# A recurrence and an ELU network in one launch: the output gate by tanh, smaller first loads, and a planner with other numbers

## The chip, the core and the metric

The kernel runs on one core of a Trainium2 chip. The core has a matrix engine (TensorE, PE in the profile; its weight loads are PEld), a vector engine (VectorE, DVE), an activation engine (ScalarE, ACT), a general one (GpSimd, POOL) and SyncE (SP), which here issues every DMA. The metric is device time of one launch in microseconds (us); less is better. Each engine works through its own queue in order; between engines the order is kept by semaphores.

## The reference

Four batches of eight heads run a gated recurrence over 768 positions of 40 channels; its output, 3072 rows of 320, goes through a two-layer network with an ELU. Cut to what matters:

```python
for t in range(S):
    m_new = np.maximum(f_gate[:, :, t] + m, i_gate[:, :, t])
    f_stab = np.exp(f_gate[:, :, t] + m - m_new)
    i_stab = np.exp(i_gate[:, :, t] - m_new)
    C = f_stab[..., None, None] * C + i_stab[..., None, None] * np.einsum('bhd,bhe->bhde', vt, kt)
    n = f_stab[..., None] * n + i_stab[..., None] * kt
    h_tilde = np.einsum('bhde,bhe->bhd', C, qt)
    denom = np.maximum(np.abs(nq), 1.0)          # nq = n . q, per head
    o = 1.0 / (1.0 + np.exp(-o_gate[:, :, t]))
    y[:, :, t] = o * h_tilde / denom
...
h = x @ w_in                                     # (3072, 320) @ (320, 2048)
g = np.where(h > 0.0, h, np.exp(np.minimum(h, 0.0)) - 1.0)
return g @ w_out                                 # (3072, 2048) @ (2048, 320)
```

The weights arrive in double precision.

## The kernel before

**Tiles.** The 768 positions are cut into six chunks of 128, and tile n is chunk c = n // 4 of batch b = n % 4, 24 tiles in all. Within a chunk the recurrence is done as attention with decays (`attention(n)`): scores of keys and queries (`products`, L597), a matrix w of decays, which for the first two chunks comes from sums of logs that PE spreads into a PSUM buffer h (`spread`, L628 to L638) and an Exp on ACT, and for later chunks from a scan on DVE (L645); w times scores (L662); outputs in PSUM (`outputs`, L682 to L700) with the state C of earlier chunks. `gate_chunk(c)` prepares the gates of one chunk for all batches, mostly on DVE. The end of a tile is a chain: Abs of the normalizer (L733, ACT), max with 1 and reciprocal (L737, L738, DVE), the sigmoid of the output gate times 1/den (L742, DVE or POOL), times the output (L746, DVE), a copy, a transpose on PE (`turn`, L763), and a split of the result into a high and a low part (xh, L769; xl, L776 or L780), because the network's matmuls work in a shorter format and sum several products. The sigmoid itself is three activations in place over 320 columns (L615): Exp of -x, Ln of 1 + that, Exp of the negative.

**Network.** `ffn` works on blocks of two or three tiles. A step is 128 of the 2048 hidden columns: eight matmuls of the first layer into an h buffer (L816), Relu and Exp on ACT (L824, L827), add and max on DVE (L829), a split (L832 on ACT, L834 on DVE or POOL), and three matmuls a tile of the second layer (L843). Steps run in a fixed order. A PSUM pool has two h buffers, used by steps, by spreads and by some weight conversions.

**Weights.** `conversion(i)` turns a piece of double-precision words, i = 0 to 17 (c0, c1, ... in the order below), into high and low parts: a load into one of three wide buffers (L322), two passes on ACT (L327, L332), three on DVE (L336, L341, L346), an add on POOL (L351), the high part by a copy on ACT (L357), the low part by DVE, POOL or by PE and a copy (L361, L369 to L373). The wide buffer is free after the add on POOL. The first step of the first block needs c0, c1 and c2 (its second layer c3), steps 2 and 3 need c4, steps 4 on c5 to c7.

**Order.** Nothing is scheduled by the chip or by the compiler. A planner (`Plan`) takes every operation with the engines that may do it, a cost in us on each, the buffers that it touches and a rank, simulates engines, one DMA queue and the pools, and writes the operations out in the order in which its simulation starts them, each on the engine on which it would end first. Ready operations go by rank, then by the longest tail of costs behind them. Its constants are HOP (delay from one engine to another), RATE (bytes per us of the DMA queue), LAND (delay of a landing) and DEEP (how far SP's issues may run ahead of the queue). FIRST gives ranks 0, 1, 2, ... to tiles (t) and conversions (c); those not named in it get a small rank from the step that needs them. An operation with "port" in its costs shares a port between DVE and POOL.

## Time and profile before

| | |
|---|---|
| median of 3 runs | 480.05 us (475.24 to 480.37) |
| profiled execution | 479.09 us, of which the span on the core is 477.1 us |
| mean granted clock of TensorE | 0.981 |
| instructions | 13768 |
| moved by DMA | 52.83 MB, 39389 packets |

The span runs from the first to the last instruction of one profiled execution. Busy time is the time in which an engine had an instruction in work; matmuls are pipelined, and at a granted clock below 1.00 the same work is busy for longer. A line such as L816 is a line of the kernel; one line may issue on different engines.

### The profile page before, as it was taken

Reading aid. Unit: us, or ns where it says so; the run is one execution under the profiler, and the core shown is the slowest. Engines: PE = TensorE matmul, PEld = TensorE weight load, DVE = VectorE, ACT = ScalarE, POOL = GpSimd, SP = SyncE. Lnnn points to the kernel's source line nnn. Section 1 sums busy time; section 2 is a strip of 40 time slices with the busy share of each in tenths; the row PEclk is TensorE's granted clock in tenths of the full one; section 3 lists DMA queues with packets and bytes.
Section 4 is the critical chain, followed back from the end, with each engine's and each line's share of the span. In section 5 each row is a group of like instructions: output and inputs, shape, how many; then the busy total and the mean of one; then the engine's idle time right before and its main releaser. Section 6 shows DMA issues by size and latency. Waiting matters only on the chain.

```text
span 477.1 us, 13768 instructions
## 1 busy us (share of the span) xinstructions
PE 456.9 (96%) x5692; PEld 428.4 (90%) x5692; DVE 347.8 (73%) x729; ACT 303.1 (64%) x743; POOL 89.5 (19%) x103
## 2 busy tenths in 40 slices
PE   5977999999999989999999999999999999999996
PEld 3645889899999989999989999999999999999996
DVE  7897899997869899638995768648875475456543
ACT  5886788897876556646465546655546564645764
POOL 2421244433213131003040122102110010000000
PEclk9796999999999999999999999999999999999999
DMA  8777465534143394113642334404432030100000
GB/s 261 259 225 233 134 214 170 153 116 153 41 137 97 105 278 138 43 40 98 185 144 71 101 94 134 133 3 139 140 101 82 1 101 1 43 1 3 28 1 27
DMA packets 39389, 52.83 MB, mean 111 GB/s; under 512 B 2880, under 2 KB 31264, under 8 KB 39328
## 3 DMA queue, kind: packets, MB, share of 16 engines
q1 hardware_dynamic: 39328, 51.97, 35.2%
q8 instruction: 44, 0.72, 0.6%
q14 instruction: 17, 0.14, 0.1%
HBM read 46.56 MB, written 5.39 MB: 109 GB/s over the span
## 4 chain that ended last, share of the span: by engine, by line
PE 80%; DVE 10%; DMA 3%; issue 2%; ACT 2%; POOL 1%; SPq 1%; DVEq 0%; ACTq 0%
PE h L816 34%; PE acc L843 32%; PE ps_a L597 4%; PE ps_a L690 3%; PE ps_a L682 2%; DMA wide<-in_w_in 2%; PE ps_a L763 1%; DMA w<-f_d 1%; PE h L628 1%; PE ps_a L700 1%; PE h L632 1%; PE h L638 1%; DVE w L645 1%; DMA bb<-b_d 1%; DVE gl L834 1%
## 5 line engine op out<-in xcount | busy, mean ns | idle before, releaser
L816 PE MATMUL h<-xh,w 128*128 128x384 f32 (+1 forms) x720 | 179.1, 323 | 0.4 <-ACT e L827 0.2
L843 PE MATMUL acc<-w,gh 128*128 128x320 f32 x768 | 173.4, 312 | 0.1
L843 PEld LDWEIGHTS acc<-w,gh 128*128 128x128 f32 x768 | 127.8, 188 | 2.4 <-ACT gh L832 0.3
L816 PEld LDWEIGHTS h<-xh,w 128*128 128x128 f32 x720 | 125.6, 189 | 2.7 <-DVE e L829 1.0
L829 DVE SCALAR_TENSOR_TENSOR e<-e,h 128x384 f32<-128x384 f32 (+1 forms) x144 | 72.5, 505 | 69.8 <-ACT e L827 69.2
L843 PE MATMUL acc<-w,gl 128*128 128x320 f32 x384 | 118.7, 309 | 0.4 <-DVE gl L834 0.4
L824 ACT ACTIVATE e<-h 128x384 f32<-128x384 f32 (+1 forms) x144 | 65.4, 454 | 78.0 <-PE h L816 74.9
L816 PE MATMUL h<-xl,w 128*128 128x384 f32 (+1 forms) x432 | 112.0, 318 | 0.0
L832 ACT CAST gh<-e 128x384 fp32r<-128x384 f32 (+1 forms) x144 | 67.7, 473 | 35.1 <-DVE e L829 34.0
L834 DVE TENSOR_TENSOR gl<-e,gh 128x384 fp32r<-128x384 f32 (+1 forms) x122 | 66.3, 547 | 32.1 <-ACT gh L832 30.2
L816 PEld LDWEIGHTS h<-xl,w 128*128 128x128 f32 x432 | 76.9, 189 | 0.0
L827 ACT ACTIVATE e<-e 128x384 f32<-128x384 f32 (+1 forms) x144 | 70.5, 490 | 4.0
L843 PEld LDWEIGHTS acc<-w,gl 128*128 128x128 f32 x384 | 72.0, 188 | 0.9 <-DVE gl L834 0.8
L834 POOL TENSOR_TENSOR gl<-e,gh 128x384 fp32r<-128x384 f32 (+1 forms) x22 | 24.4, 1115 | 109.0 <-ACT gh L832 95.6
L645 DVE TENSOR_TENSOR_SCAN w<-w,ident 128x512 f32<-128x512 f32 x32 | 39.1, 1225 | 4.6 <-DMA w<-f_d 4.6
L615 ACT ACTIVATE vko<-vko 128x320 f32<-128x320 f32 x72 | 33.5, 467 | 7.7 <-DMA vko<-in_vko 7.2
L597 PE MATMUL ps_a<-qk 40*128 40x128 f32 x384 | 31.0, 304 | 6.4 <-DMA qk<-in_qk 5.1
L351 POOL TENSOR_TENSOR narrow<-narrow,wide 128x512 int32<-128x512 int32 (+1 forms) x18 | 26.5, 1474 | 55.5 <-DVE narrow L346 25.9
L597 PEld LDWEIGHTS ps_a<-qk 40*128 40x128 f32 x384 | 25.9, 204 | 11.6 <-DMA qk<-in_qk 5.1
L662 DVE TENSOR_TENSOR w<-ps_a,w 128x512 f32<-128x512 f32 x48 | 31.6, 682 | 3.1 <-PE ps_a L597 2.7
L690 PE MATMUL ps_a<-vko,w 128*32 128x41 f32 x1536 | 20.3, 207 | 0.0
L690 PEld LDWEIGHTS ps_a<-vko,w 128*32 128x32 f32 x1536 | 18.6, 114 | 1.2 <-issue 1.1
(104 smaller groups left out, 413.9 us busy)
## 6 DMA issues: line engine op xcount, KB each, us to landing
vko<-in_vko SPq DMA_DIRECT2D x24, 484.0 KB
qk<-in_qk SPq DMA_DIRECT2D x24, 448.0 KB
w<-f_d SPq DMA_DIRECT2D x32, 256.0 KB
wide<-in_w_out SPq DMA_DIRECT2D x8, 640.0 KB
wide<-in_w_in SPq DMA_DIRECT2D x8, 512.0 KB
out<-os SPq DMA_DIRECT2D x24, 160.0 KB
bb<-b_d SPq DMA_DIRECT2D x40, 80.0 KB
sum<-os SPq DMA_DIRECT2D x8, 160.0 KB
```

Of the source, the lines that this page charges most:

```text
L597: nc.tensor.matmul(ps(two, P, HH, L)[:, j, :], kt[rows, j, :], qt[rows, j, :], start=True, stop=True,)
L615: lambda e, fn=fn, kw=kw: nc.scalar.activation(v3()[2], v3()[2], fn, **kw), (), (KS,))
L645: nc.vector.tensor_tensor_scan(a, a, ident4.rearrange("p h t -> p (h t)"), 0.0, op0=ALU.mult, op1=ALU.add)
L662: lambda e, half=half: nc.vector.tensor_mul(w(half), ps(half, P, HH, L), w(half)),
L690: nc.tensor.matmul(y[r, h, :], w()[:, i, r], va()[:, h, :], start=not opened, stop=(i == H - 1), skip_group_check=True,)
L816: nc.tensor.matmul(h(), a[g][:, fs], m, start=(i == 0), stop=(i == len(prods) - 1))
L824: op(act(N), lambda e, h=h, ff=ff: nc.scalar.activation(ff("e"), h(), AF.Relu, scale=-1.0), (KHP,), (KE,))
L827: lambda e, ff=ff: nc.scalar.activation(ff("e"), ff("e"), AF.Exp, scale=-1.0), (), (KE,))
L829: lambda e, h=h, ff=ff: nc.vector.scalar_tensor_tensor(out=ff("e"), in0=ff("e"), scalar=-1.0, in1=h(), op0=ALU.add, op1=ALU.max),
L832: op(act(N), lambda e, ff=ff: nc.scalar.copy(ff("gh", F32R), ff("e")), (KE,), (KG,))
L834: lambda e, ff=ff: eng[e].tensor_sub(ff("gl", F32R), ff("e"), ff("gh", F32R).bitcast(F32)),
L843: nc.tensor.matmul(acc(a), x[:, sl], bw[g][:, j, :], start=(f == f0 and i == 0), stop=(f == f1 - 1 and i == 2),)
```

## The change

The sigmoid is written as (1 + tanh(x/2)) / 2: one activation in place of three. The 1 is added in the instruction that multiplies by the output, the 1/2 goes into the denominator as a factor of 2, and the multiplication by 1/den comes last, on the product. The table set that ACT preloads is another one. For tiles of chunk 0 the queries and keys, which lie in 112 rows of which 80 hold data (0 to 39 and 64 to 103), are loaded as two transfers of 40 rows. The copies of xh and xl, and the copy of the low part in a conversion by PE, may go to ACT or DVE. The planner has other constants, a factor on PE's costs in the first 45 us (COLD), a hop by engine, other costs for some operations, and FIRST names another order.

```diff
-    HOP = 0.1
+    HOP = {"PE": 0.19, "POOL": 0.06, "DVE": 0.04, "ACT": 0.04, "SP": 0.04}
+    COLD = ((11.5, 1.9), (18.0, 1.0), (25.0, 1.9), (45.0, 1.25))
     LAND = 1.6
-    RATE = 235e3
-    DEEP = 3.0
+    RATE = 275e3
+    DEEP = 6.0
...
-                    end = t + o.engines[best]
+                    cost = o.engines[best]
+                    if best == "PE":
+                        cost *= next((x for until, x in self.COLD if t < until), 1.0)
+                    end = t + cost
...
-    FIRST = "t0c0c4t1c1c5t2t4c3c7c11c9"
+    FIRST = "t0c0c2c3t1t2t3t4c4c1"
...
-                op(act(n), lambda e, lo=lo: nc.scalar.copy(lo, T("h", ("lower", i), P, 4 * L)[:, 0:n]),
+                op(act(n) | two_ps(n), lambda e, lo=lo: copy(e, lo, T("h", ("lower", i), P, 4 * L)[:, 0:n]),
...
-        nc.scalar.preload_act_table_set("natural_log_exp_and_others")
+        nc.scalar.preload_act_table_set("exp_and_others")
...
-        op({"SP": 0.4}, lambda e: nc.sync.dma_start(t[0:R3], qk[b, c]),
-           (), (("qk", n, 0), ("qk", n, 1)), nbytes=R3 * 2 * HH * L * 4)
+        for two, rows in enumerate(ROWS if c == 0 else [slice(0, R3)]):
+            op({"SP": 0.4}, lambda e, rows=rows: nc.sync.dma_start(t[rows], qk[b, c, rows]),
+               (), (("qk", n, two),) if c == 0 else (("qk", n, 0), ("qk", n, 1)),
+               nbytes=(rows.stop - rows.start) * 2 * HH * L * 4)
...
-        for fn, kw in ((AF.Exp, dict(scale=-1.0)), (AF.Ln, dict(bias=1.0)), (AF.Exp, dict(scale=-1.0))):
-            op(act(H * D),
-               lambda e, fn=fn, kw=kw: nc.scalar.activation(v3()[2], v3()[2], fn, **kw), (), (KS,))
+        op(act(H * D), lambda e: nc.scalar.activation(v3()[2], v3()[2], AF.Tanh, scale=0.5), (), (KS,))
...
-            nc.vector.tensor_scalar_max(den(), den(), 1.0)
+            nc.vector.tensor_scalar(den(), den(), 1.0, 2.0, op0=ALU.max, op1=ALU.mult)
...
-        op({"port": 1, "DVE": 0.3}, denominators, (), (("den", n),))
+        op({"port": 1, "DVE": 0.41}, denominators, (), (("den", n),))
+
+        def gated():
+            return xf()[:, 0 : H * D].rearrange("p (h d) -> p h d", d=D)
+
+        op({"DVE": 0.49},
+           lambda e: nc.vector.scalar_tensor_tensor(
+               out=gated(), in0=v3()[2], scalar=1.0, in1=y3()[:, :, 0:D], op0=ALU.add, op1=ALU.mult),
+           (KY, KS), (("xf", n),))
         op(two_in(H * D),
-           lambda e: eng[e].tensor_mul(v3()[2], v3()[2], den().to_broadcast([P, H, D])),
-           (("den", n),), (KS,))
-
-        def result(e):
-            nc.vector.tensor_mul(
-                xf()[:, 0 : H * D].rearrange("p (h d) -> p h d", d=D), y3()[:, :, 0:D], v3()[2]
-            )
-
-        op({"DVE": 0.49}, result, (KY, KS), (("xf", n),))
+           lambda e: eng[e].tensor_mul(gated(), gated(), den().to_broadcast([P, H, D])),
+           (("den", n),), (("xf", n),))
...
-        op(act(3 * L), lambda e: nc.scalar.copy(xs("h"), ps("tp", P, 3, L)),
+        op(act(3 * L) | two_ps(3 * L), lambda e: copy(e, xs("h"), ps("tp", P, 3, L)),
            (KTP,), (KX + ("h", slot),))
```

The lines left out change single costs: `products` on PE from 1.25 to 1.16, `outputs` from 1.6 to 1.38, the split of the logs on DVE from 1.8 to 2.2, small fills and copies on DVE from 0.08 to 0.17, and others of that size.

## Rows read from the trace of the kernel before

**Rows 1.** The profile's page, its head and its list of busy times: busy microseconds of each engine, its share of the span, and its number of instructions.

```profile
span 477.1 us, 13768 instructions
...
PE 456.9 (96%) x5692; PEld 428.4 (90%) x5692; DVE 347.8 (73%) x729; ACT 303.1 (64%) x743; POOL 89.5 (19%) x103
```

**Rows 2.** Busy time by stretches of the span. Columns: the stretch in us, its length, then for each engine the busy us in it and its instructions, the clock of TensorE that was granted (1.00 is full speed), the mean busy share of the 16 DMA engines, and GB/s.

```profile
5.00:11.80 6.80, 6.42 (x35) 4.05 (x36) 4.66 (x17) 3.88 (x8) 0.12 (x1) 1.00 1.04 336
18.70:25.50 6.80, 6.76 (x122) 5.00 (x122) 5.65 (x14) 4.81 (x13) 2.93 (x3) 0.51 0.52 166
25.50:39.10 13.60, 8.26 (x137) 5.09 (x136) 12.93 (x34) 12.14 (x30) 3.39 (x3) 0.99 0.76 237
39.10:49.40 10.30, 8.67 (x134) 7.05 (x134) 7.52 (x19) 5.65 (x14) 2.36 (x3) 0.51 0.82 237
5.00:50.00 45.00, 36.49 (x567) 25.69 (x568) 36.16 (x93) 32.91 (x76) 11.65 (x12) 0.81 0.81 251
50.00:115.00 65.00, 64.24 (x925) 59.11 (x924) 58.95 (x121) 55.13 (x128) 24.70 (x23) 1.00 0.49 157
115.00:470.00 355.00, 352.94 (x4186) 341.00 (x4185) 247.66 (x500) 211.19 (x531) 50.92 (x57) 1.00 0.28 85
470.00:477.10 7.10, 3.25 (x20) 2.56 (x18) 1.34 (x3) 1.63 (x4) 0.00 (x0) 0.94 0.13 46
```

**Rows 3.** The timeline of the first 30 us, pieces of PE and DVE. Columns: start in us, us, engine, line, operation, out<-in, shapes and count; in brackets the idle time before it and what ended that.

```profile
5.09 2.08 PE L597 MATMUL ps_a<-qk 40*128 40x128 f32 x16 [5.09 <-DMA qk<-in_qk]
...
9.97 0.69 DVE L662 TENSOR_TENSOR w<-ps_a,w 128x512 f32<-128x512 f32 x1
...
14.94 1.16 PE L597 MATMUL ps_a<-qk 40*128 40x128 f32 x16
```

**Rows 4.** Groups of ACT's instructions by line, over the whole run and then (the last row) in the first 50 us alone. Columns: line, engine, operation, out<-in and shape, count, then busy us and mean ns of one, then idle us before them and what ended it.

```profile
L827 ACT ACTIVATE e<-e 128x384 f32<-128x384 f32 (+1 forms) x144 | 70.5, 490 | 4.0
...
L615 ACT ACTIVATE vko<-vko 128x320 f32<-128x320 f32 x72 | 33.5, 467 | 7.7 <-DMA vko<-in_vko 7.2
...
L769 ACT CAST xh<-ps_a 128x384 fp32r<-128x384 f32 x24 | 11.3, 470 | 3.4 <-PE ps_a L763 3.4
...
L236 ACT COPY os<-acc 128x320 f32<-128x320 f32 x13 | 5.3, 420 | 1.6 <-PE acc L843 1.4
...
L405 ACT ACT_TABLE_LOAD x1 | 1.3, 1283 | 0.7 <-PEq L969 0.7
...
L615 ACT ACTIVATE vko<-vko 128x320 f32<-128x320 f32 x15 | 6.9, 466 | 2.3 <-DMA vko<-in_vko 2.2
```

**Rows 5.** Groups of DVE's instructions by line, the first two over the whole run, the third in the first 50 us; columns as before.

```profile
L829 DVE SCALAR_TENSOR_TENSOR e<-e,h 128x384 f32<-128x384 f32 (+1 forms) x144 | 72.5, 505 | 69.8 <-ACT e L827 69.2
...
L746 DVE TENSOR_TENSOR xf<-ps_a,vko 128x320 f32<-128x320 f32 x24 | 11.8, 490 | 1.5 <-POOL vko L742 0.3
...
L742 DVE TENSOR_TENSOR vko<-vko,den 128x320 f32<-128x320 f32 x4 | 1.9, 484 | 0.0
```

**Rows 6.** What PE waited for between 5 and 50 us: the line that waited, the one that ended the wait, us in total, times, longest us.

```profile
PE h L628 <- DVE e L829: 3.5, 1, 3.5
PE ps_a L763 <- DVE xf L746: 2.2, 3, 0.9
PE ps_a L773 <- ACT xh L769: 1.3, 1, 1.3
```

**Rows 7.** SyncE's queue: three pieces of its timeline (start in us, us, the line that issues the transfer, out<-in), and, last, a row of its own waits between 2 and 60 us.

```profile
1.19 0.41 SPq L527 DMA_DIRECT2D qk<-in_qk  x1
...
14.48 0.33 SPq L322 DMA_DIRECT2D wide<-in_w_in  x1
...
20.45 0.33 SPq L322 DMA_DIRECT2D wide<-in_w_in  x1
...
SPq L322 <- POOL narrow L351: 25.3, 7, 6.0
```

**Rows 8.** The DMA view of 240.6 to 245.5 us: the packets by size, and the transfers issued in it with the KB of each. The loads of w write 128 rows, those of bb 40.

```profile
DMA packets 1392, 0.71 MB, mean 145 GB/s; under 512 B 52, under 2 KB 1389, under 8 KB 1391
...
w<-f_d SPq DMA_DIRECT2D x2, 256.0 KB
bb<-b_d SPq DMA_DIRECT2D x2, 80.0 KB
```

**Rows 9.** The timeline around the FFN's first steps; columns as in rows 3.

```profile
34.78 0.36 PE L816 MATMUL h<-xh,w 128*128 128x256 f32 x1
...
39.52 0.83 DVE L346 SCALAR_TENSOR_TENSOR narrow<-wide,narrow 128x640 int32<-128x640 int32 x1
...
40.27 0.41 DVE L829 SCALAR_TENSOR_TENSOR e<-e,h 128x256 f32<-128x256 f32 x1
...
40.73 0.59 PE L628 MATMUL h<-mask,ident_b 128*128 128x512 bf16 x1 [3.53 <-DVE e L829]
...
47.19 0.58 PE L816 MATMUL h<-xh,w 128*128 128x256 f32 x1
...
60.28 0.78 PE L682 MATMUL ps_a<-C,bb 104*32 104x82 f32 x32
```

**Rows 10.** What PE waited for between 115 and 470 us; columns as in rows 6. The releaser "issue" means that the engine waited for nothing that the profile shows.

```profile
PE ps_a L597 <- issue: 1.3, 1, 1.3
PE ps_a L763 <- DVE xf L746: 0.4, 1, 0.4
```

More of the change, by code (lines that the diff above doesn't have):

```diff
@@ L161, in run @@
                         waits[a] -= 1
-                        hop = 0.0 if best in a.engines and len(a.engines) == 1 else self.HOP
+                        hop = 0.0 if best in a.engines and len(a.engines) == 1 else self.HOP[best]
                         when[a] = max(when[a], end + hop)
@@ L170, in run @@
                             free_at[k] = 1e9
-                            self.last[k] = max(self.last.get(k, 0.0), end + self.HOP)
+                            self.last[k] = max(self.last.get(k, 0.0), end + self.HOP[best])
                             if not users[k]:
@@ L213, in tile_mlstm_then_elu_ffn @@
     MASKED = -(2.0**100)
-    PARTS_BY_PE = 4, (0, 1, 5, 6, )
+    PARTS_BY_PE = 4, (0, 1, 5, 6)
     TMAX = max(BLOCKS)
     WMAX = max(512, W2N * DM)
-    FIRST = "t0c0c4t1c1c5t2t4c3c7c11c9"
+    FIRST = "t0c0c2c3t1t2t3t4c4c1"
     LEAD, SPACE, LEAD_C = 4, 3, 0
@@ L349, in conversion @@
            both[1::2], (KN,))
-        op({"POOL": 0.1 + 0.0023 * n},
+        op({"POOL": 0.1 + 0.0025 * n},
            lambda e: nc.gpsimd.tensor_add(narrow(), narrow(), words()[0]),
@@ L463, in log_decay @@
                 nc.vector.tensor_scalar_max(f(), f(), LOG_MIN)
-        op({"port": 1, "DVE": 0.54 if c >= LOGS else 0.7}, log_decay, (KM,), (KF,))
+        op({"port": 1, "DVE": 0.6 if c >= LOGS else 0.84}, log_decay, (KM,), (KF,))
         op({"port": 1, "POOL": 0.4, "DVE": 0.27}, lambda e: eng[e].tensor_sub(i(), i(), m()[:, 1:]), (KM,), (KI,))
@@ L492, in parts @@
                         nc.vector.tensor_sub(lc(), lc(), part)
-            op({"port": 1, "DVE": 1.8}, parts, (), (KLC, ("lcs", c)))
+            op({"port": 1, "DVE": 2.2}, parts, (), (KLC, ("lcs", c)))
             return
@@ L511, in gate_chunk @@
         KT = ("ps_a", ("iT", c))
-        op({"PE": 0.35}, lambda e: nc.tensor.transpose(turned(), i(), ident[:BH, :BH]),
+        op({"PE": 0.24}, lambda e: nc.tensor.transpose(turned(), i(), ident[:BH, :BH]),
            (KI, ("ident", 0)), (KT,))
@@ L600, in products @@
                     )
-        op({"PE": 1.25}, products, KQ + (("w", n, "room"),), tuple(("ps_a", (n, two)) for two in range(2)))
+        op({"PE": 1.16}, products, KQ + (("w", n, "room"),), tuple(("ps_a", (n, two)) for two in range(2)))
         if c < LOGS:
-            op({"POOL": 0.2, "DVE": 0.08}, lambda e: eng[e].memset(va()[:, :, D:E], 1.0), (), (KV,))
+            op({"POOL": 0.2, "DVE": 0.17}, lambda e: eng[e].memset(va()[:, :, D:E], 1.0), (), (KV,))
         else:
@@ L611, in attention @@
                lambda e: copy(e, va()[:, :, D:E], ib), (("iT", c),), (KV,))
-        for fn, kw in ((AF.Exp, dict(scale=-1.0)), (AF.Ln, dict(bias=1.0)), (AF.Exp, dict(scale=-1.0))):
-            op(act(H * D),
-               lambda e, fn=fn, kw=kw: nc.scalar.activation(v3()[2], v3()[2], fn, **kw), (), (KS,))
+        op(act(H * D), lambda e: nc.scalar.activation(v3()[2], v3()[2], AF.Tanh, scale=0.5), (), (KS,))
         if c > 0:
-            op({"POOL": 0.22, "DVE": 0.08, "ACT": 0.2},
+            op({"POOL": 0.22, "DVE": 0.17, "ACT": 0.2},
                lambda e: copy(e, dec(), bb[0:R2, :, L - 1 : L]), KB, (("dec", n),))
@@ L657, in attention @@
             if c < NC - 1:
-                op({"POOL": 0.3, "DVE": 0.08, "ACT": 0.2},
+                op({"POOL": 0.3, "DVE": 0.17, "ACT": 0.2},
                    lambda e, half=half: copy(e, wl()[:, half::2], w(half)[:, :, L - 1]),
@@ L706, in attention @@
         KY = ("ps_a", (n, "y"))
-        op({"PE": (1.6 if c else 0.9) + (0.36 if c < NC - 1 else 0.0)}, outputs,
+        op({"PE": (1.38 if c else 0.8) + (0.32 if c < NC - 1 else 0.0)}, outputs,
            (("w", n, 0), ("w", n, 1), KV) + (KB + (("C", b),) if c else ())
@@ L766, in turn @@
                 )
-        op({"PE": 0.55}, turn, (("xf", n), ("ident", 0)), (KTP,))
-        op(act(3 * L), lambda e: nc.scalar.copy(xs("h"), ps("tp", P, 3, L)),
+        op({"PE": 0.49}, turn, (("xf", n), ("ident", 0)), (KTP,))
+        op(act(3 * L) | two_ps(3 * L), lambda e: copy(e, xs("h"), ps("tp", P, 3, L)),
            (KTP,), (KX + ("h", slot),))
@@ L775, in attention @@
                (KX + ("h", slot), ("minus", 0)), (KTP,))
-            op(act(3 * L), lambda e: nc.scalar.copy(xs("l"), ps("tp", P, 3, L)),
+            op(act(3 * L) | two_ps(3 * L), lambda e: copy(e, xs("l"), ps("tp", P, 3, L)),
                (KTP,), (KX + ("l", slot),))
```

## Prediction

> **What bounds the kernel now.** I read the page's busy line first, then the busy time by stretches, then TensorE's (PE's) waits, then the timeline at the longest of them. The reader should see four things. PE is busy 456.9 of 477.1 us [rows 1], so the whole kernel has 20.2 us of PE idle to give. The stretches say where [rows 2]: 5.1 us before the first matmul [rows 3], 45.00 - 36.49 = 8.5 us between 5 and 50, 0.8 us between 50 and 115, 2.1 us in the 355 us from 115 to 470, and 3.85 us in the tail. Third, busy is not the same as fast: the granted clock is 0.51, mostly the 1.2 GHz level, in 18.7 to 25.5 and 39.1 to 49.4. Before 11.8 the record shows 1.00, yet the 16 products of L597 took 2.08 us at 5.09 and 1.16 us at 14.94 [rows 3], so that stretch was slow too. At half speed half of the busy time is lost: 6.76/2 = 3.4 us and 8.67/2 = 4.3 us; in 5 to 11.8 it is 6.42 x (1 - 1.16/2.08) = 2.8 us. Together the first 50 us cost about 5.1 + 8.5 + 10.5 = 24 us of PE time, everything later 7. Fourth, from 115 us on VectorE (DVE) and ScalarE (ACT) are busy 70% and 59% while PE is at 99.4%: what is saved on them there is worth nothing. Any gain or loss must come from the head.
>
> The profiled execution took 479.09 us, 2.0 more than its span; the median of the runs is 480.05 with a spread of 5 us. The sum below is made against 479.1, and I treat the 1 us to the median as noise. About 1% (4.8 us) is what a measurement of this kernel can tell from no change.
>
> **The sigmoid by tanh.** Per tile three activations of L615 become one, so 48 of 72 go, at 467 ns: 22.4 us of ACT over the run [rows 4]. Only those in the head can count: 15 ran before 50 us, so 10 x 0.466 = 4.7 us go there, from an ACT that was busy 12.14 of 13.6 us in the worst stretch, 25.5 to 39.1 [rows 2]. No trace shows a tanh; its price lies between the cheapest ACT pass over 320 columns, the 420 ns copy of os, and the 490 ns of the wider pass of L827 [rows 4]. I take 467 ns, the same form with another function; the two ends differ by 0.5 us over the ten tiles or so of the head. The gated product becomes a scalar_tensor_tensor on DVE in place of the multiply of L746 (490 ns); L829, of that kind, takes 505 ns on up to 384 columns [rows 5], so nothing is added. The max gets a second operation in the same instruction and stays one instruction. The multiply by 1/den (L742, 484 ns on DVE in the head) only moves behind the gated product. In the chain of a tile Abs, max, reciprocal, multiply, product, turn, the product no longer stands behind the reciprocal, so 0.49 us leaves it. PE waited for the ends of such chains 2.2 us (xf L746) and 1.3 us (xh L769) in the head [rows 6]. Of these 3.5 us I take 1.0; bounds 0 and 3.5. The preload names another table set. The trace has one ACT_TABLE_LOAD, 1.28 us [rows 4]; I count one again, and the rival prices more. (The Trainium skill, "ScalarE: Activation LUTs", section "Table sets: the hidden batching unit", lists exp, tanh, relu and abs in one set; by it no further load comes. No run here shows it yet.)
>
> **Queries and keys without the zero rows.** For four tiles one transfer of 448 KB becomes two of 160 KB, and SyncE issues one more, 0.41 us each [rows 7]. By bytes the first products come earlier: the load took 5.09 - 1.19 = 3.9 us to use, and 128 of 448 KB are worth at most 3.9 x 128/448 = 1.1 us, less 0.41 for the second issue, so 0.7. But the trace warns that rows, not bytes, may count. Two loads of w with 128 rows and two of bb with 40 rows left 52 packets under 512 B [rows 8]. If each engine that carries a part ends it with one such packet, that is 16 + 16 + 10 + 10: a 40-row load runs on ten of the sixteen DMA engines. Then each of the ten carries 4 + 4 rows of 4 KB, where 112 rows on sixteen gave 7, so the pair is one row in seven longer, 3.9/7 + 0.41 = 1.0 us later. (That is the rule of the Trainium skill, "DMA: Bandwidth & Descriptors", section "Why a DMA increments its semaphore by 16 and not by 1": the largest number up to 16 that divides the rows; the trace agrees with 52. By it this edit loses, by the byte count it wins.) Either way the cover is the same: the products of tile 0 end at 5.09 + 2.08 = 7.17, and their reader, the first multiply of L662, starts at 9.97, behind the decay path [rows 3]. 2.8 us of slack hide -0.7 as well as +1.0. I take 0; the bounds are -0.7 and +0.5, the latter for loads of tiles 1 and 2 pushed back.
>
> **Planner's numbers, copies on either engine, order.** RATE, DEEP, HOP, COLD and the single costs add no instruction; they and FIRST decide only the order in each engine's queue. The xh, xl and difference copies (470 ns on ACT for xh [rows 4]) may go to DVE; DVE's price for a pass that reads PSUM is near, 490 ns for L746 [rows 5], so this moves work and saves none, and DVE, at 36.16 of 45 us in the head, has 8.8 us of room [rows 2]. What FIRST does can be read from the longest wait. At 40.73 tile 3's spread (L628) had waited 3.5 us for DVE's L829 [rows 6, 9]. The first step of the FFN had gone ahead at 34.78 and held one of the two h buffers; its L829 stood on DVE behind chunk 1's gates and, last, the 0.83 us of L346 at 39.52. In the new FIRST tiles 1 to 4 rank before c1, and no FFN step can run without c1, so tile 3's spread goes ahead of that step, not behind it. I count the wait as gone: -3.5 us. What is late next is c1, and with it the start of the FFN. After that wait came the second slow stretch, which cost 4.3 us. Less idle time before it may keep the clock up or not; I take half, -2.1, bounds 0 and -4.3.
>
> Against this stands the cost of c1 being last. All three wide buffers are first filled by c0, c2 and c3, so c1's load waits for a conversion to end; SyncE waited 25.3 us for just that, the add of L351 [rows 7]. In the kernel before, by the ranks, the load issued at 14.48, into the first buffer that came free, was c1's, and step 0 followed 20.3 us later, at 34.78. Now c4 ranks before c1 and takes that buffer; c1 takes the next, at 20.45 [rows 7], so by the same lag step 0 comes near 41. The second step ran at 47.19 [rows 9], so the steady feeding need not come later, but c5 to c8 are then further behind. I take +1.0 as an estimate between 0 and the rival's price.
>
> **The sum.** 479.1 - 1.0 (chains) + 0 (loads) - 3.5 (the wait) - 2.1 (clock) + 1.0 (late c1) = 473.5; I say 474. Steady state and tail: 0, because PE's waits after 115 us are one of 1.3 us for nothing that the profile shows and one of 0.4 [rows 10].
>
> **The rivals.** (a) *No net gain.* DVE was busy 58.95 of 65 us from 50 to 115 with PE never short [rows 2]: the head is balanced, and conversions put behind attention must still be done. PE's gain by 50 us is given back waiting for c5 to c8. For it: DVE is the fullest helper, and nothing in the change takes work from it. Against: its 8.8 us of idle before 50. Time: 479.1 - 1.0 = 478. (b) *Slower: c1 and c4 too late.* If the plan runs tiles 2 to 4 to their end before c1, step 0 starts when tile 4 is through, whose outputs came at 60.28 [rows 9]; even 5 us sooner that is 55 against 47.19. It decides from the point where step 0 comes later than about 47. PE then stands 8 us, less what tile 4's attention gives it meanwhile, about 5 us (an estimate: products of 1.16 [rows 3], first outputs of 0.78 [rows 9], and some 3 us for the other parts, not shown), and another slow stretch costs 4.3: 479.1 + 3 + 4.3 = 486. For it: rank 9 of 9; against: the queues fill gaps, and gaps there are. (c) *The tanh brings table loads.* Two loads of 1.28 us per tile against 0.93 saved is +1.6 us; over ten tiles, on an ACT 85% busy from 50 to 115 (55.13 of 65), 16 us, of which 9.9 fit in its idle time: 479 + 6 = 485, slower. The change would not do what it says.
>
> **How the numbers follow.** Forecast 0.52, (a) 0.33, (b) 0.12, (c) 0.03. The forecast's own range is 468 to 476: at one end the other half of the clock, the rest of the chain waits, no price for a late c1 and the better end of the loads (474 - 2.1 - 2.5 - 1.0 - 0.7), at the other half of the h wait back. For 8 in 10 I go from 464, where the slow stretch of 18.7 to 25.5 is gone too (-3.4), to 484, short of (b). The line of 1% lies at 475.3, inside the forecast's range; five sixths of the forecast and a sixth of (a) fall below it: faster 0.48. Same takes the rest of both, 0.37; slower is (b) and (c), 0.15.
>
> **What would show it.** Right: no wait of about 3.5 us of L628 for L829; PE idle below 5 us between 5 and 50; granted clock 1.00 in some of 39 to 49; 24 activations of L615's successor near 0.47 us and one table load; first matmul at 5.1 within 1 us; DVE fuller before 50. Wrong: PE idle moved to 50 to 80 with waits for L351 or the wide loads (rival a), the first L843 after 52 us (b), more table loads (c). The prediction fails if the new order makes another early op hold an h or ps_a buffer.

## The result and the profile after

The kernel after took 480.91 us (median of 20 runs, 477.3 to 486.52), the kernel before, on the same chip, 477.22 us (20 runs, 474.03 to 480.79). The ratio is 1.0069, 95% interval 1.0041 to 1.0096: 3.3 us slower, where 474 us was forecast. Times here and below are medians of all executions, while a ratio leaves out those more than 1.5% above the fastest of their kernel; the traced execution of e2 is one of these. The profiled execution took 479.62 us, the one of the kernel before 479.09: the two traces lie only 0.5 us apart, so they show where the waits stand and not the whole 3.3 us. The page's head, its busy line and the line of its packets:

```profile
span 477.8 us, 13709 instructions
...
PE 458.2 (96%) x5692; PEld 429.7 (90%) x5692; DVE 341.2 (71%) x719; ACT 282.1 (59%) x688; POOL 96.9 (20%) x120
...
DMA packets 39278, 52.32 MB, mean 109 GB/s; under 512 B 2896, under 2 KB 31280, under 8 KB 39216
```

ACT lost 21 us of work against [rows 1], and PE's idle time went from 20.2 to 19.6. By stretches (columns as in [rows 2]), after:

```profile
5.00:10.00 5.00, 4.61 (x26) 3.06 (x26) 2.80 (x11) 0.47 (x1) 0.00 (x0) 1.00 0.92 250
10.00:15.00 5.00, 1.73 (x10) 0.98 (x9) 3.36 (x6) 3.84 (x7) 1.29 (x1) 1.00 1.04 269
31.00:41.20 10.20, 9.81 (x170) 7.09 (x170) 6.64 (x22) 6.98 (x21) 1.20 (x3) 0.51 0.58 174
5.00:50.00 45.00, 37.17 (x705) 26.69 (x706) 33.69 (x85) 27.48 (x66) 11.13 (x14) 0.89 0.82 227
50.00:115.00 65.00, 63.36 (x775) 59.09 (x774) 56.70 (x121) 52.88 (x119) 19.23 (x19) 1.00 0.49 154
115.00:470.00 355.00, 353.30 (x4192) 340.45 (x4191) 245.31 (x499) 197.41 (x493) 64.31 (x78) 1.00 0.29 87
```

and two stretches of before that were not shown:

```profile
5.00:10.00 5.00, 4.62 (x27) 3.07 (x28) 3.00 (x13) 2.34 (x5) 0.00 (x0) 1.00 1.04 327
10.00:15.00 5.00, 5.00 (x125) 3.22 (x123) 3.81 (x9) 3.81 (x9) 2.63 (x3) 1.00 1.02 337
```

The new thing stands in the last two columns. The DMA engines are nearly as busy as before (0.92 and 1.04 in place of 1.04 and 1.02) and move 250 and 269 GB/s in place of 327 and 337. From 10 to 15 us PE works 1.73 us, where before it never stopped. ACT's timeline in that place:

```profile
6.59 0.47 ACT L619 ACTIVATE vko<-vko 128x320 f32<-128x320 f32 x1 [2.12 <-DMA vko<-in_vko]
10.37 0.66 ACT L331 ACTIVATE narrow<-wide 128x512 f32<-128x512 f32 x1 [3.31 <-DMA wide<-in_w_in]
...
12.39 0.66 ACT L331 ACTIVATE narrow<-wide 128x512 f32<-128x512 f32 x1 [0.80 <-DMA wide<-in_w_in]
12.96 0.58 ACT L657 ACTIVATE w<-h 128x512 f32<-128x512 f32 x1
```

In the new order the first passes of c0 and c2 (L331) stand on ACT ahead of tile 0's Exp of the decays (L657); ACT waits 3.3 us for c0's words, and the Exp starts at 12.96. PE's waits from 5 to 50 us (columns as in [rows 6]), and the timeline of PE at the second of them:

```profile
PE h L632 <- ACT w L657: 3.3, 1, 3.3
PE ps_a L694 <- issue: 2.6, 1, 2.6
PE ps_a L778 <- DVE xh L240: 1.2, 1, 1.2
PE ps_a L686 <- issue: 0.4, 1, 0.4
```

```profile
27.01 0.81 PE L694 MATMUL ps_a<-vko,w 128*32 128x41 f32 x64
27.62 0.49 PE L704 MATMUL ps_a<-vko 128*32 128x41 f32 x32
28.06 0.75 PE L694 MATMUL ps_a<-vko,w 128*32 128x41 f32 x58
31.39 0.29 PE L694 MATMUL ps_a<-vko,w 128*32 128x41 f32 x3 [2.58 <-issue]
```

The wait for DVE of [rows 6] (3.5 us) is gone. Two others stand in its place: 3.3 us for tile 0's Exp, and 2.6 us in the middle of a row of equal matmuls, for nothing that the profile shows as an event. (The records have two matmuls for each f32 matmul of the kernel.)

### The profile page after: what moved, and what is told of

Read it like the earlier page. It is cut to its first block, busy times and chain, and to the rows that moved or that the text cites. A ratio compares the mean times of both kernels' runs of the same rounds, so it can differ in the third digit from the quotient of the medians.

```text
span 477.8 us, 13709 instructions
## 1 busy us (share of the span) xinstructions
PE 458.2 (96%) x5692; PEld 429.7 (90%) x5692; DVE 341.2 (71%) x719; ACT 282.1 (59%) x688; POOL 96.9 (20%) x120
## 2 busy tenths in 40 slices
DMA packets 39278, 52.32 MB, mean 109 GB/s; under 512 B 2896, under 2 KB 31280, under 8 KB 39216
## 4 chain that ended last, share of the span: by engine, by line
PE 88%; DVE 4%; DMA 3%; ACT 2%; issue 2%; SPq 1%; ACTq 0%
PE h L821 37%; PE acc L848 36%; PE ps_a L603 5%; PE ps_a L694 3%; PE ps_a L686 3%; DMA wide<-in_w_in 2%; PE ps_a L768 2%; PE ps_a L704 1%; DMA w<-f_d 1%; DMA bb<-b_d 1%; DVE gl L839 1%; DVE w L666 0%; PE h L373 0%; DVE narrow L350 0%; PE h L632 0%
## 5 line engine op out<-in xcount | busy, mean ns | idle before, releaser
L839 DVE TENSOR_TENSOR gl<-e,gh 128x384 fp32r<-128x384 f32 (+1 forms) x130 | 69.6, 537 | 37.5 <-ACT gh L837 34.8
L603 PE MATMUL ps_a<-qk 40*128 40x128 f32 x384 | 32.6, 305 | 4.9 <-DMA qk<-in_qk 4.1
L603 PEld LDWEIGHTS ps_a<-qk 40*128 40x128 f32 x384 | 27.0, 204 | 9.8 <-DMA qk<-in_qk 4.5
L839 POOL TENSOR_TENSOR gl<-e,gh 128x384 fp32r<-128x384 f32 (+1 forms) x14 | 15.0, 1069 | 99.2 <-ACT gh L837 95.9
L720 POOL TENSOR_TENSOR C<-C,dec 40x164 f32<-40x164 f32 x22 | 12.2, 556 | 79.6 <-PE ps_a L686 78.8
L694 PE MATMUL ps_a<-vko,w 128*32 128x41 f32 x1536 | 20.5, 207 | 2.6 <-issue 2.6
```

The source lines that it names most:

```text
L603: nc.tensor.matmul(ps(two, P, HH, L)[:, j, :], kt[rows, j, :], qt[rows, j, :], start=True, stop=True,)
L694: nc.tensor.matmul(y[r, h, :], w()[:, i, r], va()[:, h, :], start=not opened, stop=(i == H - 1), skip_group_check=True,)
L839: lambda e, ff=ff: eng[e].tensor_sub(ff("gl", F32R), ff("e"), ff("gh", F32R).bitcast(F32)),
```

## The experiments

Ratios are to the kernel before on the same chip, with the 95% interval; 0.01 is 4.8 us. "The new order" is the order of instructions of the kernel after, "the old order" that of the kernel before; unless a run is said to be planned anew, each engine's queue is kept as it was but for the edit.

**Whole loads in the new order (e1).** Both ops stay in the plan; the first loads all 112 rows, the second nothing.

```diff
-            op({"SP": 0.4}, lambda e, rows=rows: nc.sync.dma_start(t[rows], qk[b, c, rows]),
+            def whole(e, two=two):
+                if two == 0:
+                    nc.sync.dma_start(t[0:R3], qk[b, c])
+            op({"SP": 0.4}, whole,
```

> The changed kernel, its planned order untouched, but the queries and keys of chunk 0 come in one transfer of 112 rows (at the place of the first of the two). Theory L (loads): the 40-row pairs slow the early DMA, so c0 lands at 10.4 us and the first exps of tile 0 stand on ScalarE behind it. Undone, DMA moves over 300 GB/s between 5 and 10 us instead of 250, the wait of 3.3 us of L632 for L657 falls below 1, and the time falls by 3 us or more, to a ratio to the kernel before of at most 1.000. Theory O (order): the new order costs by itself; the wait moves by the landing of the loads but the time stays within 1 us of the changed kernel, ratio 1.005 to 1.009.

476.75 us, ratio 0.9993 [0.9956, 1.0031]. The stretches from 5 and from 10 us, then ACT:

```profile
5.00:10.00 5.00, 4.63 (x28) 3.07 (x29) 4.22 (x14) 1.70 (x3) 0.00 (x0) 1.00 1.03 321
10.00:15.00 5.00, 3.88 (x23) 2.41 (x23) 3.88 (x10) 4.70 (x9) 2.26 (x3) 1.00 1.03 341
```

```profile
7.82 0.66 ACT L331 ACTIVATE narrow<-wide 128x512 f32<-128x512 f32 x1 [1.10 <-DMA wide<-in_w_in]
...
10.79 0.58 ACT L661 ACTIVATE w<-h 128x512 f32<-128x512 f32 x1
```

The rate is back, c0's pass comes 2.6 us sooner than in the kernel after, and 1.0069 - 0.9993 = 0.0076, 3.6 us (give or take 2.2), is the price of the smaller loads in this order.

**Why smaller loads are slower: engines or number (e2, e3).** e2 loads two times 48 rows. If each engine that carries a part ends it with one packet under 512 B, as the prediction took it, these run on all 16 engines: there are 2944 = 2880 - 4 x 16 + 8 x 16 such packets, where e1 and the kernel before have 2880 and the kernel after 2896 = 2880 - 4 x 16 + 8 x 10. e3 puts the pairs of 40 into the kernel before.

```diff
-            op({"SP": 0.4}, lambda e, rows=rows: nc.sync.dma_start(t[rows], qk[b, c, rows]),
+            some = slice(64 * two, 64 * two + 48) if c == 0 else rows
+
+            op({"SP": 0.4}, lambda e, rows=some: nc.sync.dma_start(t[rows], qk[b, c, rows]),
```

> The changed kernel with its order untouched, its pairs of 40 rows made pairs of 48 rows (8 zero rows more in each half). If what matters is that 40 rows go to ten engines, the 48 rows go to sixteen, with 3 rows in each: the packets under 512 B are 8 x 16 again for these loads, DMA between 5 and 10 us is over 300 GB/s, and the time is that of the load of 112 rows within 1 us (theory L). If what matters is the second transfer or SyncE's second issue, it is as slow as the changed kernel, ratio about 1.007. Theory O: 1.005 to 1.009 too, with fast DMA.

> The kernel before with its order untouched and only the loads of chunk 0's queries and keys cut into pairs of 40 rows, issued at the same place. Theory L: DMA between 5 and 10 us falls from 327 to about 260 GB/s, and the time rises by 1 to 4 us, ratio 1.002 to 1.008 (less than in the changed kernel, where the first conversions stand ahead of tile 0's exps). Theory O: no change, ratio 0.999 to 1.001.

e2: 481.93 us, 1.0054 [1.0005, 1.0102]; e3: 478.83 us, 1.0018 [0.9981, 1.0054]. From 5 to 10 us, e2 and e3:

```profile
5.00:10.00 5.00, 4.62 (x26) 3.06 (x27) 2.80 (x11) 0.47 (x1) 0.00 (x0) 1.00 0.98 257
```

```profile
5.00:10.00 5.00, 4.50 (x25) 2.95 (x26) 2.80 (x11) 1.89 (x4) 0.00 (x0) 1.00 1.01 217
```

So it isn't the ten engines: sixteen are as slow. Nor is it that SyncE issues more and the engines wait for it, for they are busy all the time (0.98 and 1.01). (The rule by which the prediction counted ten, from the Trainium skill, "DMA: Bandwidth & Descriptors", section "Why a DMA increments its semaphore by 16 and not by 1", agrees with both counts of packets; the later landing worked out from it did not come.) In the old order the transfers are as slow, but no loss can be measured (up to 0.54% is not excluded). That this order has the slack that the prediction counted on fits that; no run shows the slack itself.

**One pair, and another pair taken away (e11, e12).** e11: a pair for tile 0 alone, tiles 1 to 3 whole. e12: whole loads, and also the two 64-row loads of c2 and of c11 made one of 128 rows, from an input with these rows side by side.

```diff
-               lambda e, s=s, a=a: nc.sync.dma_start(wide()[s].bitcast(I64), a),
+               lambda e, s=s, a=a, j=j: (
+                   nc.sync.dma_start(wide()[s].bitcast(I64), a) if len(src) == 1
+                   else nc.sync.dma_start(wide().bitcast(I64), w_in2[convs[i][3] // 8]) if j == 0 else None),
```

> The kernel after's order, in which only tile 0's queries and keys come as a pair of 40 rows; those of tiles 1 to 3 come whole. If the first pair alone puts the DMA engines out of step for what follows: GB/s in 5 to 10 us near 250 to 270 (after: 250, e1: 321), c0's first pass near 10 us, ratio 1.003 to 1.007. If each pair slows only itself and what is beside it: 5 to 10 us near 310 to 325 GB/s, c0's first pass near 7.5 us, first product near 4.1 us, ratio .997 to 1.001.

> The kernel after's order with whole 112-row loads, and the two conversions whose words come as two loads of 64 rows (c2 and c11) get them by one load of 128 rows, from an input laid out for it. If any pair of partial loads slows the transfers (also pairs of 64 rows, which use 16 engines): GB/s in 5 to 10 us above e1's 321, near 335, c2's first pass 0.5 to 1 us sooner than e1's 10.22, ratio .994 to .999 against e1's .9993. If only the pairs of queries and keys do it, ahead of everything else: within 5 GB/s of e1, c2's pass within 0.3 us, ratio .997 to 1.002.

e11: 482.53 us, 1.011 [1.0067, 1.0153]; e12: 477.61 us, 1.0007 [0.9976, 1.0038]. From 5 to 10 us, e11 and e12:

```profile
5.00:10.00 5.00, 4.65 (x26) 3.06 (x26) 2.80 (x11) 0.47 (x1) 0.00 (x0) 1.00 1.01 254
```

```profile
5.00:10.00 5.00, 4.61 (x27) 3.06 (x28) 4.65 (x16) 3.02 (x6) 0.06 (x1) 1.00 1.04 408
```

The first pair alone lowers the rate, and taking away a pair that the kernel before had too gives 408 GB/s in place of 321, at the same busy share and with the same packets but for 32 small ones (39358 for 39390): packets take longer behind a pair. Tile 0's Exp starts at 9.25 in e12 (e1: 10.79), yet the time doesn't follow: PE then stood 3.5 us in the wait called issue (in e11 4.1, which is part of its higher time), and the clock was halved from 23.0 to 36.7.

**Does the price go through ACT's queue (e9, e10)?** The order is kept, but the conversions that stood ahead of tile 0's two Exps are emitted right behind them; with whole loads (e9) and with pairs of 40 (e10).

```diff
+            if first and (getattr(o, "conv", False) or any(y[3] in o.before for y in held)):
+                held.append(x)
+                continue
...
```

> The kernel after with whole 112-row loads (as in e1), its order kept, except that every conversion operation on ACT, DVE and POOL that stood ahead of tile 0's two Exps of the decays now stands right behind them. In e1 ACT stood in L331 for c0 and c2 from 6.7 to 10.8 us and the first Exp came at 10.79, where the kernel before had it at 9.07. Theory M (the wait of ACT in the conversions ahead of tile 0 is what costs the head its early start): first Exp near 9.1 us, PE 10 to 15 near 5 us (e1: 3.9, before: 5.0), the granted clock at 1.00 from 12 to 15 us (e1: 20.5), ratio to before .985 to .995. Rival (the gain is given back, because c0 and c2 come later and the FFN's first step with them): first Exp near 9.1 too, but PE 15 to 50 lower than in e1 by what was won, ratio .996 to 1.004. Ratio over 1.008: the conversions, not the attention, are what the head waits for.

> The same hold with the pairs of 40-row loads of the kernel after. In the kernel after ACT waited 3.3 us for c0's load at 10.37 and the first Exp came at 12.96, PE 10 to 15 was 1.73 us. If the price of the pairs goes through ACT's queue (a late conversion load stops tile 0's Exps): first Exp near 9 us, PE 10 to 15 above 4 us, and the ratio to before within .004 of the same hold with whole loads. If it goes through everything that is loaded later (weights and the values of tiles 1 to 3 some 3 us behind): first Exp near 9 us as well, but the ratio stays .007 to .01 above the whole loads', as between the kernel after and e1 (1.0069 against .9993).

e9: 477.93 us, 0.9999 [0.9962, 1.0037]; e10: 480.44 us, 1.0063 [1.0029, 1.0097]. In both the Exp starts where it did before the change, at 9.06 and 9.07. It gains nothing, and the 0.0064 between whole loads and pairs stays (give or take 0.005): ACT's wait is the place where the late words show first, not the only way by which they cost. What else is late shows in the products of tile 1, in e9 and in e10:

```profile
13.36 1.16 PE L622 MATMUL ps_a<-qk 40*128 40x128 f32 x16 [1.33 <-DMA qk<-in_qk]
```

```profile
15.03 0.79 PE L618 MATMUL ps_a<-qk 40*128 40x128 f32 x2 [2.77 <-DMA qk<-in_qk]
16.37 2.04 PE L618 MATMUL ps_a<-qk 40*128 40x128 f32 x14 [0.56 <-DMA qk<-in_qk]
```

With ACT out of the way PE waits for the next late transfer, tile 1's own queries and keys: 3.3 us with pairs, 1.3 with whole loads. My theory that the head loses by ACT's queue fell.

**The order without the tanh, the tanh without the order (e5, e4).** e5 is e1 with the three activations; e4 is the kernel before with one, the 1 added where 1/den is multiplied in (on POOL by a second instruction), so that the order of the chain stays as it was.

```diff
-        op(act(H * D), lambda e: nc.scalar.activation(v3()[2], v3()[2], AF.Tanh, scale=0.5), (), (KS,))
+        def sigmoid(e):
+            for fn, kw in ((AF.Exp, dict(scale=-1.0)), (AF.Ln, dict(bias=1.0)), (AF.Exp, dict(scale=-1.0))):
+                nc.scalar.activation(v3()[2], v3()[2], fn, **kw)
+        op(act(H * D), sigmoid, (), (KS,))
...
```

> The changed kernel's order on every engine, with the loads of 112 rows and the sigmoid of three activations of the kernel before at the place of the tanh: the planner's numbers, FIRST and the copies on either engine alone. If order and tanh each are worth next to nothing, ratio 0.998 to 1.003. If tanh is worth what I predicted for it (1 us) and the order eats it, 1.000 to 1.005. If the order alone is worth the 4.6 us of my sum, 0.990 or less.

> The kernel before with its order untouched and only the gate by tanh: one activation at the place of the first of the three, nothing at the places of the other two; the addition of 1 in the multiplication by 1/den (where that runs on GpSimd, a second instruction there). One table load. My prediction's price: 4.7 us of ScalarE less before 50 us, about 1 us of time, ratio 0.996 to 1.000. If ScalarE's load in the head is what binds, 3 us or more, ratio below 0.994.

e5: 485.49 us, 1.0167 [1.0111, 1.0224]; e4: 476.88 us, 0.9995 [0.9952, 1.0038]. One pass in place of three is worth nothing measurable in the old order and 1.0167 - 0.9993 = 0.0174, 8 us, in the new one, which was planned with one pass on ACT. The order alone costs 8 us. In the traced execution part of that is clock: e5 from 30.6 to 51.1,

```profile
30.60:51.10 20.50, 19.92 (x309) 14.83 (x310) 13.56 (x33) 14.08 (x37) 5.04 (x7) 0.50 0.54 173
```

half of 19.92 us lost, where e1 has one such stretch of 6.8 us. But the clock does not carry the 8 us. Over e5's six executions the mean granted clock went from 0.977 to 1.000, and the one at 1.000 still took 484.78 us, 7.2 above the kernel before on that chip (477.61). By which wait the order loses without the tanh isn't shown.

**New plans (e6, e8).** The planner run again with whole loads: e6 also makes the conversions of c0, c2 and c3 wait for tile 0's Exps; e8 goes back to the old FIRST with all the new numbers.

```diff
-    FIRST = "t0c0c2c3t1t2t3t4c4c1"
+    FIRST = "t0c0c4t1c1c5t2t4c3c7c11c9"
```

> The changed kernel with loads of 112 rows, planned anew with one more dependency: the first two ScalarE passes of conversions 0, 2 and 3 come after tile 0's two exps. Theory M (the exps of tile 0 behind passes whose loads have not landed starve TensorE from 10 to 14 us, and with that its clock stays low until 20 us): tile 0's first exp starts near 9.1 us instead of 10.8, no wait over 0.5 us of the next spread for it, granted clock 1.00 by 13 us, time 3 us below the run with 112 rows alone, ratio 0.990 to 0.995. Rival: later steps are bound by VectorE and the conversions, and the gain of the start is given back: 0.997 to 1.002.

> The changed kernel with loads of 112 rows and FIRST of the kernel before, planned anew with the new numbers. If FIRST is what brings or costs time, this differs by 2 us or more from the run with 112 rows and the new FIRST; the wait of tile 3's spread for L829 of 3.5 us should come back, and tile 0's exps again stand ahead of the conversions or not as the plan has them. If the numbers of the planner decide, ratio 0.997 to 1.002 as there.

e6: 484.26 us, 1.0149 [1.0099, 1.0198]; e8: 487.87 us, 1.0223 [1.017, 1.0276]; e6 with pairs of 40 (e7): 486.32 us, 1.0195 [1.0144, 1.0246]. e6 has the good start (PE busy 5.00 us from 10 to 15) and loses later: 7.63 us of PE in 50 to 60, and three stretches of half clock. Each new plan moves the time by more than the edits under study (7 to 11 us), so these runs say little about them; e9 and e10, which keep the order, do.

**What the wait called issue is (e13, e14).** In e1, e12 and the kernel after PE stands still at the same place. While it does, the view of DMA by queue (packets, MB, share) shows, beside the data, a packet of another queue (after, 28.5 to 30 us):

```profile
q8 instruction: 1, 0.02, 5.5%
```

Over the whole run this queue moves 45 packets in e1, one for some 253 of PE's 11384 matmuls and weight loads; in e14 below, which has 640 of them fewer, it moves 42:

```profile
q8 instruction: 45, 0.74, 0.6%
```

```profile
q8 instruction: 42, 0.69, 0.7%
```

e13 puts 32 small matmuls of zeros into PE's idle start; e14 writes the state (L708) by 8 matmuls of 40 rows a tile in place of 16 of 32 and 8. Both are otherwise e1.

```diff
+    idle = const.tile([P, P], BF16, name="idle")
+    nc.vector.memset(idle, 0.0)
+    for _ in range(32):
+        nc.tensor.matmul(T("h", ("idle",), P, 64), idle, idle[:, 0:1].to_broadcast([P, 64]), start=True, stop=True)
```

```diff
-                        for a, z in ((0, 32), (32, D)):
+                        for a, z in ((0, D),):
```

> The kernel after with whole 112-row loads (as e1), and 32 matmuls of 128x64 zeros with their 32 weight loads on PE at the very start, where it waits 4 to 5 us for the first queries and keys; nothing reads them. (1) If the wait called issue is PE's instructions arriving late, it comes again at PE's 705th record, now 64 records of real work earlier: some 30 matmuls sooner in the second tile's outputs, for 1.5 to 3.5 us. If it hangs on that work (a buffer, a load), it stands where it stood in e1, 3 matmuls before the end of L698's second group, at the 769th record. (2) If the slow clock of the first 20 us comes from the idle start, the clock is at 1.00 before 10 us and the first 16 products of L607 take less than the 2.08 us; ratio .985 to .995 then. If it hangs on what comes later, it goes up near 20 us as in e1 and the ratio stays .997 to 1.002.

> The kernel after with whole 112-row loads (as e1), in which the state's matmuls (the last ones of outputs, L708) write 40 rows at once instead of 32 and 8: 8 matmuls a tile in place of 16, on 20 tiles. If the wait called issue is late instructions, it comes after the same count of records, 705, which is now 32 to 64 records of old work later, in the second tile's L708 or behind its end, and is shorter, under 1.5 us; ratio .992 to .998. If it hangs on the work it stays where it was, 2.0 us. If 40 rows at once take longer than 32 and 8 beside each other, L708's busy time goes up from the 0.49 us a tile and the ratio is 1.000 to 1.004.

e13: 485.06 us, 1.0136 [1.0095, 1.0178]; e14: 480.75 us, 1.0055 [1.0021, 1.0089]. All that PE had done when it stood still, in e1, e12 and e13, one row each (matmuls and weight loads in brackets):

```profile
0.00:27.10 27.10, 19.70 (x348) 13.33 (x349) 22.20 (x56) 16.77 (x36) 8.80 (x18) 1.00 0.92 289
```

```profile
0.00:25.00 25.00, 17.43 (x348) 11.97 (x349) 21.30 (x56) 16.98 (x37) 8.44 (x18) 0.96 0.94 312
```

```profile
0.00:28.00 28.00, 21.21 (x348) 14.79 (x349) 21.89 (x58) 17.52 (x38) 8.99 (x18) 1.00 0.95 279
```

348 and 349 each time (347 and 348 in the kernel after), with 32 of each idle ones in e13. The expectations call the next one the 705th record; by these rows it is the 698th. In e13 the wait came 32 matmuls earlier in the real work, in the middle of the second tile's outputs,

```profile
26.62 0.46 PE L698 MATMUL ps_a<-vko,w 128*32 128x41 f32 x27
30.33 0.53 PE L698 MATMUL ps_a<-vko,w 128*32 128x41 f32 x35 [3.25 <-issue]
```

and three more came later, one of 0.9 on L690 and two of 6.0 together on L708; in all 10.2 us of such waits against e1's 2.9, a difference of 7.3 us, where the times differ by 0.0143, 6.8 us. In e14, with 64 records fewer ahead of it, the same groups run through:

```profile
26.45 0.81 PE L698 MATMUL ps_a<-vko,w 128*32 128x41 f32 x64
27.20 0.51 PE L708 MATMUL ps_a<-vko 128*40 128x41 f32 x16
```

So the wait hangs on how many instructions PE has used up, not on its work: PE's instructions come late. (That they come in blocks over a DMA queue is told by the Trainium skill, "Runtime: NRT & Kernel Launch", section "Instruction fetch mechanics", which calls the cost mostly hidden; here it is 1.9 us in e5 and e9 to 4.1 in e11.) Where the pairs slow the data it is longer: 2.6 us in the kernel after against 2.0 in e1, 2.3 in e10 against 1.9 in e9. The new order sets the outputs of two tiles back to back, 192 matmuls in the records within some 2.4 us without the wait, and the count falls there. The slow clock of the start, read from equal matmuls (0.63 us before it ends, 0.38 behind), did not move in e13: up at 20.7 us, as in e1 at 20.5. So 1.9 us of matmuls in PE's idle start do not bring it up. e14 is still 3.0 us slower than e1, though it lacks a wait of 2.0: L698's groups now take 0.75 us to the first of L708 (26.45 to 27.20), where in the kernel after it was 0.61 (27.01 to 27.62); over 20 tiles that is some 2.8 us, an estimate. Three waits that e1 does not have follow at once, 0.7 and 0.9 us for ACT's copy of the state C and 0.9 for a multiply on DVE (L670), 2.5 together.

**Without that wait (e16, e17).** As e13 with 60 matmuls in front, on e1 and on e12.

> As e13 (the kernel after with whole 112-row loads, matmuls of zeros in PE's idle start), with 60 matmuls and their loads in place of 32: 120 records in front. The 705th record then falls on what was the 585th, the end of the first of the two tiles' outputs that stand back to back, and the packet is asked for some 100 records sooner, near 22 us of e1, ahead of PE's wait for DVE at 23.8. If the wait is set by the time from that request: under 1.5 us at the 705th record, where e1 had 2.0 and e13 3.3. The later bursts get other boundaries too; with no more than e1's 2.9 us of issue waits in all, the ratio is .993 to 1.001; with as many as e13's 10.2, 1.010 to 1.016.

> The same 120 records in front of e12 (the kernel after with whole 112-row loads and whole loads of c2 and c11), which lost 3.5 us to the wait at the 705th record and had the slow clock from 23.0 to 36.7. If that wait was what let the clock fall: no wait over 1.5 us at the 705th record, a slow stretch of 10 us or less, ratio .986 to .995 (e12: 1.0007). If the clock falls anyway: .995 to 1.002. With new waits later as in e13: over 1.005.

e16: 480.33 us, 1.0068 [1.0034, 1.0102]; e17: 477.15 us, 1.0013 [0.9984, 1.0042]. The wait is gone as expected (issue 0.9 and 0.4 us in all) and the time is no better. What was behind it, in e16:

```profile
28.08 0.48 PE L607 MATMUL ps_a<-qk 40*128 40x128 f32 x2
30.26 1.16 PE L607 MATMUL ps_a<-qk 40*128 40x128 f32 x14 [1.70 <-ACT C L240]
...
32.33 0.55 PE L772 MATMUL ps_a<-ident,xf 128*128 128x128 f32 x3 [0.91 <-ACT C L240]
33.75 0.90 PE L772 MATMUL ps_a<-ident,xf 128*128 128x128 f32 x3 [0.87 <-DVE w L670]
```

The next tile's products need the buffer that ACT frees by copying the state, behind DVE's gated product of the tile before. In e1, whose wait called issue ends at 29.06, and in e12 no such wait is listed. These three come to 3.5 us in e16, where e1 stood 2.0 in the wait called issue, and to 3.4 in e17, where e12 stood 3.5: the waits lay one under the other. That is 1.5 us of the 3.6 by which e16 is slower than e1; the rest stays open.

**Whole loads of c2 in the old order (e15, e18).** e15 is the kernel before with e12's edit; e18 has the tanh too.

> The kernel before with one change: c2 and c11 get their words by one load of 128 rows in place of two of 64. If paired loads slow what is beside them in this order too: 5 to 10 us above 380 GB/s (before: 327), c2's first pass sooner by 1 us or more; whether it shows in the time hangs on the slack, which e3 found wide in this order (ratio of the slower loads 1.0018): ratio .994 to 1.000. If it holds only behind the new order's loads: 320 to 340 GB/s and .998 to 1.002.

> The kernel before with the output gate by tanh (as e4, .9995) and whole loads of c2 and c11 (as e15, .9961), in the old order. If the two add up: .993 to .998. If the faster words only move the waits for instructions about (e15 had 3.5 us of them after 115 us, the kernel before 1.3): .998 to 1.004.

e15: 476.5 us, 0.9961 [0.9923, 0.9998], with 409 GB/s from 5 to 10 us: the lowest ratio of all, though not clear of e1's 0.9993 and e4's 0.9995. e18: 480.51 us, 1.0068 [1.0032, 1.0103]; the two don't add. Its profiled execution took 1111.72 us, where the other eleven took 474.93 to 482.16, so its trace can't be read beside the others and why is open.

## Why the prediction was wrong

By the runs the change divides into the order, +8.0 us (e5), the tanh in that order, -8.3 (e1 against e5), and the pairs, +3.6 (after against e1): +3.3. Each carries 2 to 3 us of uncertainty. Order and tanh together are -0.3 [-2.1, +1.5] (e1), where the sum had -1.0 - 3.5 - 2.1 + 1.0 = -5.6. So two steps failed: the wait and the clock, counted as 5.6 us gained and worth nothing here, and the loads, put at 0, which cost 3.6. The base took 1.9 us of this back (477.22 for 479.1).

**The loads: the step that failed by its cover.** The prediction asked when the first products would come and who reads them, and bounded the edit by -0.7 and +0.5. The products did begin 1.0 us sooner, at 4.09, against the row count that spoke for later, but only the first of them; they ended at 7.07 in place of 7.17, with their reader not waiting. The cost of 3.6 us is not on that path at all. It lies on what comes next on the same DMA engines: c0's words (10.37 for 7.82), tile 1's queries and keys (3.3 us of PE's time in e10), PE's own instructions (2.6 for 2.0). How the 3.6 us divide among these isn't shown. "The cover is the same" was true of the transfer and false of its neighbours; the bound of +0.5 for loads pushed back named the right thing at a seventh of its size. In the old order (e3) no loss was measured.

**The wait of the spread: right, and worth nothing.** The 3.5 us went, for the reason given: the FFN's first step no longer stands ahead of tile 3's spread. But "what is late next" was answered with c1. What was late next is tile 0's Exp, 3.3 us, and PE's own instructions, 2.6 us, and behind these the copy of the state (1.7 us in e16). PE's idle time from 5 to 50 us is 7.8 against 8.5 us, where below 5 was the sign of being right.

**The clock: -2.1 was nothing.** The stretch of 39.1 to 49.4 moved to 31.0 to 41.2, 9.81/2 = 4.9 us; the slow start lasted to 20.8 instead of 11.8, with 12.93 us of busy time from 4.09, by the prediction's own measure 12.93 x (1 - 1.16/2.08) = 5.7. Together 10.6 against 10.5 in the two traces: the slow stretches after the start lost 2.8 us less, as was hoped, and the start 2.9 more.

**The tanh: right in its own terms, wrong in standing alone.** There was one table load of 1.28 us, and 24 activations of 470 ns, where 467 was taken. (The Trainium skill, "ScalarE: Activation LUTs", section "Table sets: the hidden batching unit", lists exp and tanh in one set; the one load agrees.) DVE's gated product took 484 ns, where the prediction had 490 to 505:

```profile
L619 ACT ACTIVATE vko<-vko 128x320 f32<-128x320 f32 x24 | 11.3, 470 | 13.1 <-DMA vko<-in_vko 13.1
...
L409 ACT ACT_TABLE_LOAD x1 | 1.3, 1283 | 0.7 <-PEq L974 0.7
```

```profile
L750 DVE SCALAR_TENSOR_TENSOR xf<-vko,ps_a 128x320 f32<-128x320 f32 x24 | 11.6, 484 | 8.7 <-ACT den L737 6.6 <-PE ps_a L704 1.7
```

(The two ends of its price, 420 and 490 ns, lie 0.7 us apart over ten tiles, not 0.5.) The -1.0 stood for the shorter chain, and no run has that by itself: PE's waits for the ends of chains fell from 3.5 us [rows 6] to 1.2 (L778), in another order, and e4 (-0.2 +- 2) tests the two passes saved alone. That the order needs the lighter ACT, and loses 8 us without it, stood nowhere in the sum: parts were priced one by one against an order that only one of them had.

**c1: the sign of rival (b), not its price.** The first step's DVE operation came at 59.69, where [rows 9] has 40.27 and the sum meant about 46:

```profile
59.69 0.42 DVE L834 SCALAR_TENSOR_TENSOR e<-e,h 128x256 f32<-128x256 f32 x1
```

PE stood only 65 - 63.36 = 1.6 us between 50 and 115: it had done 705 matmuls from 5 to 50, where the kernel before did 567, and attention filled the time. Rival (a), no net gain, is what order and tanh came to, by another way than it said: not c5 to c8, but waits that lay one under the other (e14, e16, e17). The pairs then made it slower, which no rival named.

**The base.** The three runs shown had a median of 480.05, the twenty beside the kernel after 477.22. The forecast was 0.987 of the one, and would have been 471 of the other.

## What to carry to other kernels

Price a transfer that is cut in two by what queues behind it on the same engines, and not only by its own reader. Before counting a wait as gained, list all that is next to end there, the engine's own instructions among them: a wait that stands at the same count of instructions, whatever work is put in front, is not a dependency, and taking it away may only show the one beneath. An order written out for one set of costs is not a part to be added to the others: test it with the costs that it was made for and without.

## What the runs showed of the hardware

Two transfers in place of one slow the transfers behind them at nearly the same busy share (0.92 to 1.04): 321 to 250 GB/s for pairs of 40 rows, 257 for pairs of 48 on 16 engines, and 321 to 408 when a pair of 64 rows becomes one of 128. How the packets get in each other's way isn't shown. PE stood 1.9 to 4.1 us where its instructions ran out within a burst of small matmuls, at the same count (347 or 348 matmuls) in every kernel with the same order and no matmuls put in front. And 3.4 us of matmuls of zeros at the start (e16) left the clock's first rise at about 19.5 us, against 20.5.
